# The up-projection's inputs in another column order: feed-forward units by 96-token block, residue and 24 tokens

## The chip, the cores and the metric

The kernel runs on one core of one Trainium2 chip. The metric is the device time of one execution in microseconds (us), lower is better. The engines of a core have queues of their own and work side by side: PE (TensorE, the matmuls; its weight loads, PEld, overlap them), DVE (VectorE), ACT (ScalarE), POOL (GpSimd, which here issues the loads) and SP (SyncE, which here issues the stores and the DMA transposes). Each works through its queue in order.

## The reference

Attention for 8 batches and 8 heads over 576 positions of 64 channels, and a feed-forward block on its 4608 tokens:

```python
mask_plain = (rel >= 0) & (rel < 32)                         # heads 0 to 3
mask_dil = (rel >= 0) & (rel < 128) & (rel % 4 == 0)         # heads 4 to 7
attn = softmax(q @ k.T / 8, under the head's mask) @ v
x = attn.transpose(0, 2, 1, 3).reshape(4608, 512)
a = x @ w1                 # 512 -> 1024
b = x @ w2
out = ((a * b) @ w3) @ w_out
```

`rel` is the query's position less the key's. The inputs are float32; the kernel works in bfloat16 and adds up in float32.

## The kernel before

A batch of attention has four steps (`Step(b, u, hf)`): u = 0 are the plain heads, u = 1 the dilated ones, and hf is a half of the six query blocks of 96. For u = 1 the positions stand by residue modulo 4 (144 of each), so that a dilated window becomes a plain one. A step is: scores on PE (L351, tile `sp`; the two interleaved halves `c` of the 64 channels make a step of two elements between columns of `qt` and `kt`), exponentials on ACT (L361), a mask on DVE (L367; in the first two batches a bias matmul instead, L338), values on PE (L384, tile `vo`), reciprocal and normalisation on DVE (L402, L408, tile `xo`), and a transpose into `XT`: by PE and ACT in batches 0 and 1 (`back`, `keep`), by a DMA transpose from batch 2 on (`back_dma`). `turn` transposes the loaded q, k (and early v) on DVE: in one piece for plain heads (L286), in two for dilated ones (L299), where the write sorts the positions by residue. In batches 0 and 1 `v_back` and `v_keep` bring v into place; later v is loaded in place and `halo_v` (L224) copies the overlap. `band` and `blocks` make the bias at the start, `masks_of_bias` the masks.

`XT[u]` holds, for each partition (two heads of 64 channels), the attention's output: block, head pair, 96 columns. The columns of u = 0 are in the order of the sequence, those of u = 1 by residue.

The feed-forward block works in 16 units of 288 tokens (half a batch: residues 0 and 1, or 2 and 3), each with 8 pairs of groups. A group (`up`, L454, tile `ab`) is four matmuls of 288 columns, one for each 128 of the 512 input channels, in the order `ORDER = (2, 3, 0, 1)`: channels 2 and 3 are of `XT[1]`, 0 and 1 of `XT[0]`. Since a unit is half of the residues, `unit_cols` reads channels 0 and 1 with every fourth column. The first group of a pair is copied by ACT (`copy_a`, L465), the second multiplied with it by DVE (`gate`, L470) into the ring `gt`. `down` (L481, tile `y`) takes 128 tokens of `gt` through w3 @ w_out, which the kernel multiplies once (`w3_back` L511, `w3_keep` L518, `w3_mul` L523, `w3_done` L533); `copy_y` and `store` end the work.

The order on each engine is planned before the program is written: `Plan` runs tasks with given durations and ranks (`RANK`, added to ten times the batch) and takes the ready task of lowest rank. The order found stays fixed. A group is planned at 490 ns. `paced` holds the attention's steps back to about 2.25 batches ahead of the feed-forward block. Where pairs of groups run dry of attention output, or an engine's queue has another task in front, the engine waits.

Of the kernel before, what the change touches and what calls it, by code (L numbers as in the profile page):

```python
# [133 lines left out]
def kernel(  # L134
# [112 lines left out]
    def band():  # L247

        base, mid = bias[:, 1, :], bias[:, 5, QB // 2 : QB]
# [12 lines left out]

    def blocks():

        base = bias[:, 1, :]
        nc.vector.tensor_copy(out=bias[:, 0:5:4, :], in_=base.unsqueeze(1).to_broadcast([P, 2, QB]))
# [3 lines left out]
        nc.vector.tensor_copy(out=bias[:, 6, :], in_=base)  # L270

# [51 lines left out]
    class Step:  # L323
# [8 lines left out]
        def scores(self, biased=False):  # L332
# [12 lines left out]
            for mm in range(3):  # L345
                m = 3 * hf + mm
                for c in range(2):
                    for g in range(4):
                        prt = slice(32 * g, 32 * g + 32)
                        qq = qt[prt, u, QB * m : QB * m + QB, c]  # L350
                        nc.tensor.matmul(  # L351
                            out=self.sp[:, g, QB * mm : QB * mm + QB],
                            lhsT=kt[prt, u, QB * m : QB * m + P, c],
                            rhs=qq,
                            start=(c == 0 and not biased),
                            stop=(c == 1 and (mm == 2 or not biased)),
                        )
# [34 lines left out]
        def recip(self, pg=None):  # L392
            if pg in (None, 0):
                self.rcp = wk_pool.tile([P, 4, 3], F32, tag="rcp", bufs=4, name="rcp")
                self.xo = wk_pool.tile([P, 3, 4, D], BF16, tag="xo", bufs=4, name="xo")
            if pg is None:
# [9 lines left out]
        def norm(self, pg):  # L406
            gs = slice(2 * pg, 2 * pg + 2)
            nc.vector.tensor_tensor(  # L408
                out=self.xo[0:QB, :, gs, :].rearrange("p m g d -> p g m d"),
                in0=self.o[pg][0:QB, :, :, 0:D],  # L410
                in1=self.rcp[0:QB, gs, :].unsqueeze(3).to_broadcast([QB, 2, 3, D]),
                op=AL.mult,
            )

        def cols(self):
            m0 = self.b * BLK + 3 * self.hf
            return XT[self.u][:, m0 : m0 + 3, :, :]

        def back(self):
            self.x = bank([P, 3, 2, QB], BF16, "x")  # L420
            for mm in range(3):
                for pg in range(2):
                    nc.tensor.transpose(  # L423
                        out=self.x[:, mm, pg, :],
                        in_=self.xo[0:QB, mm, 2 * pg : 2 * pg + 2, :],
                        identity=ident[0:QB, 0:QB],
                    )

# [3 lines left out]
        def back_dma(self):  # L432
            nc.sync.dma_start_transpose(
                out=self.cols().rearrange("p m g x -> p (m g) x"),
                in_=self.xo[0:QB, :, :, :].rearrange("p m g d -> p (m g d)"),
            )
# [31 lines left out]
    def gate(k, f):  # L468
        c0 = (k * UNIT) % RING
        nc.vector.tensor_tensor(  # L470
            out=gt[:, f, c0 : c0 + UNIT],
            in0=held[("b", k, f)],
            in1=held[("s", k, f)],
            op=AL.mult,
# [122 lines left out]
    bnd = add("band", "DMA", (700, 0), [c0], band, 2.6, lat=-1800)  # L597
    blk = add("blocks", "DVE", 900, [bnd], blocks, 0, lat=80)
    mk = add("masks", "DVE", 700, [blk], masks_of_bias, 40, lat=80)
# [30 lines left out]
    for b in range(B):  # L630
# [9 lines left out]
        if fast:  # L640
            vals = {}
            for u in range(2):
                tv = turns(b, u, "vn", 10 * b + RANK["T"])
                for half in range(2):
# [4 lines left out]
                    vals[(u, half)] = [  # L649
                        add(f"VK{b}.{u}", eng, 1000, [x, c0],  # L650
                            lambda b=b, u=u, h=half, e=eng: v_keep(b, u, h, e), 10 * b + RANK["VK"], lat=100)
                    ]
        else:
            hal = add(f"HALO{b}", "DVE", 450, LV[b], lambda b=b: halo_v(b), 10 * b + 2, lat=80)
            vals = {(u, h): [hal] + LV[b] for u in range(2) for h in range(2)}
        kept[b], vdone[b] = [], []
        for i in range(4):
# [7 lines left out]
            else:  # L665
                s = add("S" + n, "PE", 480, T[u], st.scores, b - 99 + RANK["S"], after=[prev["s"]])
                e = add("E" + n, "ACT", 1150, [s], st.exps, 10 * b + RANK["E"], lat=100, after=[prev["e"][i]])
                m = add("M" + n, "DVE", 680, [e, mk], st.masks, 10 * b + 2, lat=80)
            paced.append((b, i, s))
            prev["s"] = e  # L670
            ns, rc = [], None
            for pg in range(2):
                vv = add(f"V{n}.{pg}", "PE", 220, [m] + vals[(u, hf)],
                         lambda st=st, pg=pg: st.values(pg), b - 99 + RANK["V"], slot=True)
                rc = add(f"R{n}.{pg}", "DVE", 160, [vv], lambda st=st, pg=pg: st.recip(pg), 10 * b + RANK["N"],
                         lat=0, after=[prev["x"][i], rc])
                ns.append(add(f"N{n}.{pg}", "DVE", 520, [vv, rc], lambda st=st, pg=pg: st.norm(pg),
                              10 * b + RANK["N"], lat=80))
# [16 lines left out]
    def ups(k, f):  # L695
# [14 lines left out]
                 slot=True, after=[a])  # L710
        G[(k, f)] = add("G", "DVE", 453, [bb, ca], lambda: gate(k, f), -1, lat=100)
        gates.append(G[(k, f)])
# [64 lines left out]
```

## Time and profile before

| | |
|---|---|
| runs | 332.85, 333.99, 334.31 us; median 333.99 |
| profiled execution | 333.33 us |
| its span, first to last instruction | 331.5 us |
| mean granted TensorE clock | 0.99 |
| software DMA queue, share of 16 engines' span | 46.0% |
| hardware DMA queue | 18.3% |
| HBM read, written | 38.80 MB, 9.44 MB |

The profile is of one execution. Busy time is the time in which an engine had an instruction at work; a wait is the idle time before an instruction, with what ended it. A group of instructions is told by its line in the kernel, its engine and the tiles it writes and reads (`out<-in`).

### The profile page before, as it was taken

Reading aid. Unit: us, or ns where it says so; the run is one execution under the profiler, and the core shown is the slowest. Engines: PE = TensorE matmul, PEld = TensorE weight load, DVE = VectorE, ACT = ScalarE, POOL = GpSimd, SP = SyncE. Lnnn points to the kernel's source line nnn. Section 1 sums busy time; section 2 is a strip of 40 time slices with the busy share of each in tenths; the row PEclk is TensorE's granted clock in tenths of the full one; section 3 lists DMA queues with packets and bytes.
Section 4 is the critical chain, followed back from the end, with each engine's and each line's share of the span. In section 5 each row is a group of like instructions: output and inputs, shape, how many; then the busy total and the mean of one; then the engine's idle time right before and its main releaser. Section 6 shows DMA issues by size and latency. Waiting matters only on the chain.

```text
span 331.5 us, 6739 instructions
## 1 busy us (share of the span) xinstructions
PE 318.3 (96%) x2706; PEld 177.4 (54%) x2736; DVE 173.0 (52%) x373; ACT 126.5 (38%) x231; POOL 61.5 (19%) x98
## 2 busy tenths in 40 slices
PE   6789999989999999999999999999999999999995
PEld 2565555555555555555555555555555555555552
DVE  5862326997878777876766454444442221222220
ACT  1562254376354333343343332433332232222222
POOL 8413522135432501061122000000000000000000
PEclk9699999999999999999999999999999999999999
DMA  7999999849997959599955131221303110101112
GB/s 111 201 207 208 211 211 130 124 89 149 153 127 122 156 89 159 116 170 143 87 72 69 49 51 50 74 59 29 72 3 81 32 34 36 61 28 35 34 32 95
DMA packets 58030, 32.81 MB, mean 99 GB/s; under 512 B 44688, under 2 KB 47760, under 8 KB 58000
## 3 DMA queue, kind: packets, MB, share of 16 engines
q0 software_dynamic: 37776, 19.40, 46.0%
q1 hardware_dynamic: 20224, 12.98, 18.3%
q8 instruction: 21, 0.34, 0.4%
q14 instruction: 9, 0.07, 0.1%
HBM read 38.80 MB, written 9.44 MB: 145 GB/s over the span
## 4 chain that ended last, share of the span: by engine, by line
PE 92%; DVE 2%; DMA 2%; ACT 2%; issue 1%; POOL 0%; POOLq 0%; ACTq 0%
PE ab L454 59%; PE y L481 18%; PE wf L523 4%; PE sp L351 3%; PE vo L384 3%; DMA vn<-in_v_dram 2%; DVE xo L408 1%; PE sp L338 1%; PE x L511 1%; PE vx L308 1%; ACT et L361 1%; PE x L423 1%; DVE vt L286 0%; ACT asb L465 0%; ACT osb L492 0%
## 5 line engine op out<-in xcount | busy, mean ns | idle before, releaser
L454 PE MATMUL ab<-XT,w_sb 128*128 128x288 bf16 x1024 | 205.1, 360 | 1.2 <-ACT XT L430 0.7
L454 PEld LDWEIGHTS <-w_sb 128*128 128x128 bf16 x1024 | 103.5, 104 | 73.6 <-issue 1.3
L470 DVE TENSOR_TENSOR gt<-ab,asb 128x288 bf16<-128x288 f32 x128 | 58.5, 457 | 123.6 <-PE ab L454 122.8
L465 ACT CAST asb<-ab 128x288 bf16<-128x288 f32 x128 | 51.0, 398 | 107.7 <-PE ab L454 107.2
L481 PE MATMUL y<-wf_sb,gt 128*128 128x512 bf16 x261 | 66.5, 382 | 1.3
L481 PEld LDWEIGHTS <-gt 128*128 128x128 bf16 x288 | 29.3, 102 | 35.3
L492 ACT COPY osb<-y 128x512 f32<-128x512 f32 x36 | 21.1, 585 | 68.4 <-PE y L481 62.1
L361 ACT ACTIVATE et<-sp 128x1152 bf16<-128x1152 f32 x32 | 36.3, 1133 | 15.6 <-PE sp L351 15.4
L217 POOL DMA_DIRECT2D vp<-in_v_dram x48 | 30.3, 637 | 40.5 <-PE vo L384 22.7
L408 DVE TENSOR_TENSOR xo<-vo,rcp 96x384 bf16<-96x384 f32 x64 | 35.0, 551 | 2.1 <-DVE rcp L402 0.2
L384 PEld LDWEIGHTS <-et 128*128 128x128 bf16 x384 | 16.2, 100 | 7.9 <-ACT et L361 1.4
L384 PE MATMUL vo<-vp,et 128*128 128x65 bf16 x384 | 18.0, 197 | 1.4 <-DVE rcp L402 0.6
L367 DVE TENSOR_TENSOR et<-et,mask 128x1152 bf16<-128x1152 bf16 x24 | 17.8, 746 | 0.0
L351 PEld LDWEIGHTS <-kt 32*128 32x128 bf16 x768 | 9.8, 95 | 14.4 <-issue 11.6
L402 DVE RECIPROCAL rcp<-vo 96x6 f32<-96x6 f32 x64 | 11.4, 181 | 9.2 <-PE vo L384 9.1
L351 PE MATMUL sp<-qt,kt 32*128 32x96 bf16 x768 | 14.5, 206 | 0.5 <-DVE kt L286 0.5
L523 PE MATMUL wf<-wo_sb,w3T 128*128 128x512 bf16 x61 | 14.8, 379 | 0.2
L286 DVE STREAM_TRANSPOSE qt<-qn 128x576 uint32<-128x576 uint32 x8 | 10.0, 1246 | 2.9 <-DMA qn<-in_q_dram 2.9
L299 DVE STREAM_TRANSPOSE kt<-kn 128x320 uint32<-128x320 uint32 (+1 forms) x16 | 10.9, 681 | 0.7 <-PE sp L351 0.6
L299 DVE STREAM_TRANSPOSE qt<-qn 128x320 uint32<-128x320 uint32 (+1 forms) x16 | 10.9, 680 | 0.4 <-DMA qn<-in_q_dram 0.2
L518 ACT COPY w3T<-x 128x1024 bf16<-128x1024 bf16 x8 | 8.1, 1012 | 7.1 <-PE x L511 7.0
L195 POOL DMA_DIRECT2D kn<-in_k_dram x9 | 6.0, 671 | 23.7 <-DVE kt L299 22.7
(48 smaller groups left out, 113.7 us busy)
## 6 DMA issues: line engine op xcount, KB each, us to landing
qn<-in_q_dram POOLq DMA_DIRECT2D x7, 576.0 KB, 7.7
kn<-in_k_dram POOLq DMA_DIRECT2D x7, 576.0 KB, 6.9
w_sb<-in_moe_w_dram POOLq DMA_DIRECT2D x4, 512.0 KB, 13.4
w3n<-in_moe_w_dram POOLq DMA_DIRECT2D x8, 256.0 KB, 14.5
out_dram<-osb SPq DMA_DIRECT2D x8, 256.0 KB, 2.4
out_dram<-osb SPq DMA_DIRECT2D x8, 224.0 KB, 2.5
vp<-in_v_dram POOLq DMA_DIRECT2D x6, 288.0 KB, 8.1
out_dram<-osb SPq DMA_DIRECT2D x8, 192.0 KB, 2.3
```

The lines of the kernel that those rows point to most:

```text
L217: nc.gpsimd.dma_start(out=vp[32 + p0 : 32 + p0 + n, 4:8, m, 0:D], in_=v_rows(b, 4, 4 * t0 + res, [[4 * D, n], [S * D, 4], [1, D]]),)
L299: nc.vector.transpose(out=o, in_=i)
L351: nc.tensor.matmul(out=self.sp[:, g, QB * mm : QB * mm + QB], lhsT=kt[prt, u, QB * m : QB * m + P, c], rhs=qq, start=(c == 0 and not biase ...
L361: nc.scalar.activation(out=ev, in_=self.sp[:, :, 0:VC], func=ACT.Exp, scale=scale)
L384: nc.tensor.matmul(out=self.o[g // 2][:, g % 2, mm, :], lhsT=self.et[:, c0 : c0 + P], rhs=vp[:, 4 * self.u + g, 3 * self.hf + mm, 0 : D + ...
L408: nc.vector.tensor_tensor(out=self.xo[0:QB, :, gs, :].rearrange("p m g d -> p g m d"), in0=self.o[pg][0:QB, :, :, 0:D], in1=self.rcp[0:QB, ...
L454: nc.tensor.matmul(out=ps, lhsT=w_sb[:, c, f * P : (f + 1) * P], rhs=unit_cols(k, c), start=(j == 0), stop=(j == DCH - 1),)
L465: nc.scalar.copy(out=a_sb, in_=held[("a", k, f)])
L470: nc.vector.tensor_tensor(out=gt[:, f, c0 : c0 + UNIT], in0=held[("b", k, f)], in1=held[("s", k, f)], op=AL.mult,)
L481: nc.tensor.matmul(out=y, lhsT=gt[:, f, c0 : c0 + P], rhs=wf_sb[:, f, :], start=(f == 0), stop=(f == KFF - 1),)
L492: nc.scalar.copy(out=o_sb, in_=held[("y", i)])
L523: nc.tensor.matmul(out=ps, lhsT=w3T[ft][:, g, :], rhs=wo_sb[:, g, :], start=(g == 0), stop=(g == KFF - 1),)
```

## The change

- The unit's 288 columns are ordered by block of 96 tokens, then residue, then 24 tokens. For u = 0 the query's columns are sorted by residue within a block: `turn` takes q of the plain heads in two pieces, as for the dilated ones, and the scores read `qt` in four runs of 24. `XT[0]` then holds, in each block, the residues one after another, and a unit reads 48 neighbouring columns in each of six blocks.
- For u = 1, `XT[1]` holds one step as a whole (288 columns for each head pair), and a unit reads it as six blocks of two residues of 24 columns. `xo` is written in an order to match: by block, then head, for u = 0; by head pair, block and head for u = 1. `cols`, `back`, `keep` and `back_dma` take a step as 576 flat columns.
- `gate` writes the product back into token order in `gt`: its output is in runs of 24.
- The bias of the plain heads is sorted likewise; `blocks` goes from DVE to ACT, with a memset (`no_halo`) left on DVE.
- One more of the four value copies of batches 0 and 1 goes from ACT to DVE (`VKE`).
- `RANK` and planned durations are other numbers, which only set the order.

```diff
-RANK = dict(E=1.5, VK=2, K=1, N=0.5, T=3, VT=0.4, S=0.1, V=0.4, X=0.4)
+RANK = dict(E=2, VK=1.5, K=1.5, N=0.5, T=3, VT=0.1, S=0.3, V=0.3, X=0.3)
-VKE = (0, 0, 0, 1)
+VKE = (0, 0, 1, 1)
...
-    XT = [const.tile([P, B * BLK, 2, QB], BF16, name=f"XT{u}") for u in range(2)]
+    XT = [
+        const.tile([P, B * BLK, 2, QB], BF16, name="XT0"),
+        const.tile([P, 2 * B, 2, VC], BF16, name="XT1"),
+    ]
...
-        base = bias[:, 1, :]
-        nc.vector.tensor_copy(out=bias[:, 0:5:4, :], in_=base.unsqueeze(1).to_broadcast([P, 2, QB]))
+        base = bias[:, 6, :]
+        by_res = base.rearrange("p (t r) -> p r t", r=4)
+        nc.scalar.copy(
+            out=bias[:, 0:4, :].rearrange("p i (r t) -> p i r t", r=4),
+            in_=by_res.unsqueeze(1).to_broadcast([P, 4, 4, 24]),
+        )
+        nc.scalar.copy(out=bias[:, 4, :], in_=base)
+        nc.scalar.copy(out=bias[:, 5, 0 : QB // 2], in_=base[:, 0 : QB // 2])
+
+    def no_halo():
         nc.vector.memset(bias[0:32, 0:5:4, :], -BIG)
-        nc.vector.tensor_copy(out=bias[:, 2:4, :], in_=base.unsqueeze(1).to_broadcast([P, 2, QB]))
-        nc.vector.tensor_copy(out=bias[:, 5, 0 : QB // 2], in_=base[:, 0 : QB // 2])
-        nc.vector.tensor_copy(out=bias[:, 6, :], in_=base)
...
-                        qq = qt[prt, u, QB * m : QB * m + QB, c]
+                        if u == 0:
+                            qq = qt[prt, u, :, c].rearrange("p (r t) -> p r t", r=4)
+                            qq = qq[:, :, 24 * m : 24 * m + 24]
+                        else:
+                            qq = qt[prt, u, QB * m : QB * m + QB, c]
...
+            if self.u == 0:
+                dst = self.xo[0:QB, :].rearrange("p (m g d) -> p g m d", m=3, g=4)[:, gs, :, :]
+            else:
+                dst = self.xo[0:QB, :].rearrange("p (q m g d) -> p q g m d", q=2, m=3, g=2)
+                dst = dst[:, pg, :, :, :]
...
         def cols(self):
-            m0 = self.b * BLK + 3 * self.hf
-            return XT[self.u][:, m0 : m0 + 3, :, :]
+            if self.u == 0:
+                m0 = self.b * BLK + 3 * self.hf
+                return XT[0][:, m0 : m0 + 3, :, :].rearrange("p m g x -> p (m g x)")
+            return XT[1][:, 2 * self.b + self.hf, :, :].rearrange("p g x -> p (g x)")
...
     def unit_cols(k, c):
         b, hf = k // 2, k % 2
-        x = XT[c // 2][:, b * BLK : (b + 1) * BLK, c % 2, :]
         if c < 2:
-            x = x.rearrange("p m (t r) -> p r m t", r=4)
-            return x[:, 2 * hf : 2 * hf + 2, :, :]
-        return x[:, 3 * hf : 3 * hf + 3, :]
+            return XT[0][:, b * BLK : (b + 1) * BLK, c, 48 * hf : 48 * hf + 48]
+        return XT[1][:, k, c - 2, :].rearrange("p (r m t) -> p m r t", r=2, m=BLK)
...
-            out=gt[:, f, c0 : c0 + UNIT],
-            in0=held[("b", k, f)],
-            in1=held[("s", k, f)],
+            out=gt[:, f, c0 : c0 + UNIT].rearrange("p (r m t) -> p m r t", r=2, m=BLK),
+            in0=held[("b", k, f)].rearrange("p (m r t) -> p m r t", r=2, m=BLK),
+            in1=held[("s", k, f)].rearrange("p (m r t) -> p m r t", r=2, m=BLK),
...
-        parts = (None,) if u == 0 else (0, 1)
+        parts = (None,) if u == 0 and nm != "qn" else (0, 1)
...
-                x = add("XD" + n, "SP", 100, ns, st.back_dma, 0, lat=3000)
+                x = add("XD" + n, "SP", 100, ns, st.back_dma, 0, lat=3700)
```

The order of instructions at two places. First DVE at the start of the program, before (`qt`, `kt`, `vt` are the turned q, k and v of batch 0, `bias` the band of the early batches):

```order
L286 STREAM_TRANSPOSE qt_93<-qn 128x18x32
L266 COPY bias<-bias 128x2x96
L267 MEMSET bias 32x2x96
L268 COPY bias<-bias 128x192
L269 COPY bias<-bias 128x48
L270 COPY bias<-bias 128x96
L286 STREAM_TRANSPOSE kt_91<-kn 128x18x32
L286 STREAM_TRANSPOSE vt_95<-vn 128x18x32
```

And DVE at the same place of the changed kernel:

```order
L309 STREAM_TRANSPOSE qt_93<-qn 128x5x32x2
L309 STREAM_TRANSPOSE qt_93<-qn 128x4x32x2
L296 STREAM_TRANSPOSE kt_91<-kn 128x18x32
L280 MEMSET bias 32x2x96
L283 TENSOR_SCALAR mask<-bias 128x672
L296 STREAM_TRANSPOSE vt_95<-vn 128x18x32
```

The copies of the bias have left DVE, q comes in two pieces, and the memset and the mask stand between k and v.

Second DVE at the end of batch 1's attention, just before batch 2's first mask, before (`rcp` and `xo` are reciprocal and normalisation of one half step, `gt` a gate, `vp<-vp` batch 2's halo):

```order
L402 RECIPROCAL rcp<-vo 96x6
L408 TENSOR_TENSOR xo<-vo,rcp 96x2x3x64
L286 STREAM_TRANSPOSE kt_91<-kn 128x18x32
L299 STREAM_TRANSPOSE kt_91<-kn 128x5x32x2
L224 COPY vp_84<-vp_84 32x8x5x64
L299 STREAM_TRANSPOSE kt_91<-kn 128x4x32x2
L470 TENSOR_TENSOR gt<-ab,asb 128x288
L367 TENSOR_TENSOR et_87<-et_87,mask 128x1152
L470 TENSOR_TENSOR gt<-ab,asb 128x288
```

And in the changed kernel:

```order
L489 TENSOR_TENSOR gt<-ab,asb 128x6x2x24
L416 RECIPROCAL rcp<-vo 96x6
L427 TENSOR_TENSOR xo<-vo,rcp 96x2x3x64
L489 TENSOR_TENSOR gt<-ab,asb 128x6x2x24
L416 RECIPROCAL rcp<-vo 96x6
L427 TENSOR_TENSOR xo<-vo,rcp 96x2x3x64
L416 RECIPROCAL rcp<-vo 96x6
L427 TENSOR_TENSOR xo<-vo,rcp 96x2x3x64
L227 COPY vp_84<-vp_84 32x8x5x64
L381 TENSOR_TENSOR et_87<-et_87,mask 128x1152
```

Gates now stand between the normalisations of batch 1, where before they came behind them. On PE, 96 up-projection matmuls stand ahead of the weight fusion instead of 100, 24 instead of 8 between the first scores of batch 1 and of batch 2, and 420 instead of 432 from there to the third step of batch 6.

More of the change, by code (lines that the diff above doesn't have):

```diff
@@ L247, in band @@
     def band():
-        base, mid = bias[:, 1, :], bias[:, 5, QB // 2 : QB]
+        base, mid = bias[:, 6, :], bias[:, 5, QB // 2 : QB]
         nc.gpsimd.affine_select(
@@ L415, in cols @@
         def cols(self):
-            m0 = self.b * BLK + 3 * self.hf
-            return XT[self.u][:, m0 : m0 + 3, :, :]
+            if self.u == 0:
+                m0 = self.b * BLK + 3 * self.hf
+                return XT[0][:, m0 : m0 + 3, :, :].rearrange("p m g x -> p (m g x)")
+            return XT[1][:, 2 * self.b + self.hf, :, :].rearrange("p g x -> p (g x)")
         def back(self):
[L420 to L427, printed above, removed]
+            self.x = bank([P, 6 * QB], BF16, "x")
+            for i in range(6):
+                nc.tensor.transpose(
+                    out=self.x[:, i * QB : (i + 1) * QB],
+                    in_=self.xo[0:QB, i * P : (i + 1) * P],
+                    identity=ident[0:QB, 0:QB],
+                )
         def keep(self):
@@ L597 @@
     bnd = add("band", "DMA", (700, 0), [c0], band, 2.6, lat=-1800)
-    blk = add("blocks", "DVE", 900, [bnd], blocks, 0, lat=80)
+    blk = add("blocks", "ACT", 1200, [bnd], blocks, 0, lat=100)
+    blk = add("no halo", "DVE", 150, [blk], no_halo, 0, lat=80)
     mk = add("masks", "DVE", 700, [blk], masks_of_bias, 40, lat=80)
@@ L649 @@
                     vals[(u, half)] = [
-                        add(f"VK{b}.{u}", eng, 1000, [x, c0],
+                        add(f"VK{b}.{u}", eng, 1250, [x, c0],
                             lambda b=b, u=u, h=half, e=eng: v_keep(b, u, h, e), 10 * b + RANK["VK"], lat=100)
@@ L653 @@
         else:
-            hal = add(f"HALO{b}", "DVE", 450, LV[b], lambda b=b: halo_v(b), 10 * b + 2, lat=80)
+            hal = add(f"HALO{b}", "DVE", 820, LV[b], lambda b=b: halo_v(b), 10 * b + 2, lat=80)
             vals = {(u, h): [hal] + LV[b] for u in range(2) for h in range(2)}
@@ L667 @@
                 e = add("E" + n, "ACT", 1150, [s], st.exps, 10 * b + RANK["E"], lat=100, after=[prev["e"][i]])
-                m = add("M" + n, "DVE", 680, [e, mk], st.masks, 10 * b + 2, lat=80)
+                m = add("M" + n, "DVE", 750, [e, mk], st.masks, 10 * b + 2, lat=80)
             paced.append((b, i, s))
@@ L674 @@
                          lambda st=st, pg=pg: st.values(pg), b - 99 + RANK["V"], slot=True)
-                rc = add(f"R{n}.{pg}", "DVE", 160, [vv], lambda st=st, pg=pg: st.recip(pg), 10 * b + RANK["N"],
+                rc = add(f"R{n}.{pg}", "DVE", 181, [vv], lambda st=st, pg=pg: st.recip(pg), 10 * b + RANK["N"],
                          lat=0, after=[prev["x"][i], rc])
-                ns.append(add(f"N{n}.{pg}", "DVE", 520, [vv, rc], lambda st=st, pg=pg: st.norm(pg),
+                ns.append(add(f"N{n}.{pg}", "DVE", 551, [vv, rc], lambda st=st, pg=pg: st.norm(pg),
                               10 * b + RANK["N"], lat=80))
@@ L710, in ups @@
                  slot=True, after=[a])
-        G[(k, f)] = add("G", "DVE", 453, [bb, ca], lambda: gate(k, f), -1, lat=100)
+        G[(k, f)] = add("G", "DVE", 460, [bb, ca], lambda: gate(k, f), -1, lat=100)
         gates.append(G[(k, f)])
```

8 lines of the change are left out of this document (4 added, 4 removed).

## The prediction

> **What bounds the kernel now.** I read the page first, then the busy time by stage, then the matrix engine's instructions one line at a time. The page says which engine fills the span (columns: busy us, share of the span, instructions), and which line fills that engine:
>
> ```profile
> span 331.5 us, 6739 instructions
> PE 318.3 (96%) x2706; PEld 177.4 (54%) x2736; DVE 173.0 (52%) x373; ACT 126.5 (38%) x231; POOL 61.5 (19%) x98
> L454 PE MATMUL ab<-XT,w_sb 128*128 128x288 bf16 x1024 | 205.1, 360 | 1.2 <-ACT XT L430 0.7
> L481 PE MATMUL y<-wf_sb,gt 128*128 128x512 bf16 x261 | 66.5, 382 | 1.3
> L470 DVE TENSOR_TENSOR gt<-ab,asb 128x288 bf16<-128x288 f32 x128 | 58.5, 457 | 123.6 <-PE ab L454 122.8
> L465 ACT CAST asb<-ab 128x288 bf16<-128x288 f32 x128 | 51.0, 398 | 107.7 <-PE ab L454 107.2
> ```
>
> PE is the bound: 318.3 of 331.5 us, 205.1 of it in the up-projections of L454, and the readers of its result (gate on DVE, copy on ACT) spend 123 and 107 us waiting for it. But busy is not the same as fast. So next, what one matmul costs. These pieces are from the chain of waits (start, us, what) in the last stage, where PE has nothing but up- and down-projections, and from the timeline of PE (start, us from the first start to the last end):
>
> ```profile
> 302.09 7.60 PE ab L454 x40
> 300.36 1.73 PE y L481 x8
> 300.18 1.91 PE L481 MATMUL y<-wf_sb,gt 128*128 128x512 bf16 x8
> 7.69 0.65 PE L338 MATMUL sp<-bias,ident 128*128 128x288 bf16 x4 [1.35 <-DVE bias L270]
> 8.80 0.44 PE L351 MATMUL sp<-qt,kt 32*128 32x96 bf16 x24 [0.46 <-DVE kt L286]
> L338 PE MATMUL sp<-bias,ident x32: 282/286/448, 7.7 to 69.3; 128*128 128x288 bf16 x32
> L454 PE MATMUL ab<-XT,w_sb x1024: 283/360/440, 22.4 to 321.8; 128*128 128x288 bf16 x171
> ```
> The last two rows are of the views of one line: minimum, median and maximum of one matmul's recorded duration, in ns.
>
> Forty up-projections take 7.60 us: 190 ns each, 760 for a group of four (one output, four channels of 128 inputs). A down-projection of 512 columns takes 1.73/8 = 216 ns, 0.42 ns a column, so 288 columns should take 122. The bias matmuls have exactly that form, 288 columns read in one run: four in 0.65 us, of which the last one's duration is 0.286, so (0.65 - 0.286)/3 = 122. So 760 is not the price of 288 columns. L454 shows two populations: its minimum, 283, is the bias matmul's 282; its maximum is 440; and the median, 360, lies in the gap halfway between, as it must if half of the matmuls are of each kind. The code has the halves: channels 2 and 3 (dilated heads) are read in three runs of 96 columns, channels 0 and 1 (plain heads) in twelve runs of 24 with a step of four elements, 8 bytes. If the first two cost 2 x 122 = 244, the other two cost 516, or 258 each, 2.1 times the price.
>
> **By stage.** The span cut at the first up-projection, the first weight-fusion transpose, the first scores of batch 1, of batch 2, and of the third step of batch 6; then L454 alone in the same stretches:
>
> ```profile
> 0.00:22.40 22.40, 16.30 (x219) 9.96 (x220) 16.29 (x47) 10.29 (x17) 11.69 (x26) 0.85 1.02 169
> 22.40:41.60 19.20, 19.20 (x106) 10.86 (x106) 5.67 (x13) 5.32 (x13) 7.77 (x12) 1.00 1.16 209
> 41.60:60.50 18.90, 18.74 (x134) 10.71 (x136) 9.26 (x13) 8.89 (x10) 4.43 (x7) 1.00 1.15 152
> 60.50:75.30 14.80, 13.65 (x236) 8.88 (x239) 14.01 (x31) 10.13 (x19) 4.68 (x7) 1.00 0.71 123
> 75.30:197.40 122.10, 121.00 (x1183) 67.22 (x1200) 87.92 (x181) 49.60 (x87) 32.97 (x48) 1.00 0.94 115
> 197.40:331.50 134.10, 129.41 (x841) 69.77 (x852) 39.85 (x90) 42.30 (x86) 0.00 (x0) 1.00 0.17 47
> ...
> 22.40:41.60 19.20, 19.11 (x100) 10.40 (x99) 1.00 1.16 209
> 41.60:60.50 18.90, 1.86 (x9) 0.77 (x8) 1.00 1.15 152
> 60.50:75.30 14.80, 1.81 (x8) 0.64 (x8) 1.00 0.71 123
> 75.30:197.40 122.10, 88.10 (x433) 42.41 (x432) 1.00 0.94 115
> 197.40:331.50 134.10, 94.20 (x477) 49.10 (x476) 1.00 0.17 47
> ```
> Columns of the first six: length, busy PE, PEld, DVE, ACT, POOL with their counts, PE's granted clock, DMA share, GB/s. In the second, third, fifth and sixth stage PE is full. In the fourth, DVE is: 14.01 of 14.8 us, 95%. The up-projections stand almost wholly in stages 2, 5 and 6.
>
> **The price of the new read.** After the change channels 0 and 1 are read in six runs of 48 columns, channels 2 and 3 in twelve runs of 24, all with neighbouring elements. Lower end for a group: 4 x 122 = 488. A group that waits at its head pays a little more: the eight y matmuls of the timeline row span 1.91 us, while seven spacings of 0.216 and one duration of 0.382 make 1.89, so some 20 ns. With that, 510. If a group pays it at its head and at its tail, 533. I take 510: the wait stands in both kernels, and the tail's share was seen only behind a stepped read. Against 760 that saves 250 ns a group, 64 us over 256 groups, where PE is what ends last. Does a change of run cost anything? Three runs (L454's 283) against one (L338's 282) say no, to 1 ns; twelve are not in the trace, except with the step.
>
> Here a rule speaks against the change. The Trainium skill, "SBUF — State Buffer", section "Door 1: The DMA port swizzle", says that SBUF has lines of 16 bytes and that two hits in a line give full bandwidth, so that bf16 may be read with a step of up to eight elements for free. By it the 8-byte step costs nothing and the change would save nothing. The trace disagrees: the stepped matmuls are those that take twice as long. Should the rule hold all the same, it must be the twelve runs that cost, and that is a rival below.
>
> What the trace says of steps: the scores (L351) read their columns with a step of two elements, 4 bytes; 24 of them in four concurrent row groups take 0.44 us with the last one's tail of 0.2, so six in turn take 0.24, 40 ns for 96 columns, the full 0.42 ns. So 4 bytes are free. The scores of plain heads now read four runs of 24 with that same step: from nothing to double, 16 steps x 0.24 = 3.8 us; I take nothing, by the step.
>
> **The rest of the change, part by part.** DVE's rows:
>
> ```profile
> L286 DVE STREAM_TRANSPOSE qt<-qn 128x576 uint32<-128x576 uint32 x8 | 10.0, 1246 | 2.9 <-DMA qn<-in_q_dram 2.9
> L299 DVE STREAM_TRANSPOSE qt<-qn 128x320 uint32<-128x320 uint32 (+1 forms) x16 | 10.9, 680 | 0.4 <-DMA qn<-in_q_dram 0.2
> L321 DVE COPY vp<-vx 128x256 bf16<-128x256 bf16 x6 | 2.2, 419 | 0.7 <-PE vx L308 0.7
> L408 DVE TENSOR_TENSOR xo<-vo,rcp 96x384 bf16<-96x384 f32 x64 | 35.0, 551 | 2.1 <-DVE rcp L402 0.2
> 6.72 0.20 DVE L266 COPY bias<-bias 128x192 bf16<-128x192 bf16 x1
> 7.50 1.24 DVE L286 STREAM_TRANSPOSE kt<-kn 128x576 uint32<-128x576 uint32 x1
> ```
> - The plain heads' q is turned in two pieces: 2 x 0.680 for 1.246, +0.11 us in each of 8 batches.
> - The gate writes twelve runs of 24. Norm writes six runs of 64 for 384 elements in 551 ns, gate 288 in 457: 0.98 ns per element between them, with no sign of a price per run. I take 0; should a run cost 5 ns it is 60 ns x 128 = 7.7 us on DVE.
> - Norm writes another order, transposes and keeps the same sizes: nothing. The whole-step DMA transposes write the same 576 columns a partition as now, one piece either way: nothing.
> - Three more value copies on DVE per early batch (+1.26 us there, ACT relieved); the bias blocks (7.50 - 6.72 = 0.8 us of DVE) go to ACT, idle then. The halo memset now stands behind the k transpose, and the first scores' bias matmuls behind it; they waited till 7.69 and PE had the scores at 8.80. Now q's two pieces, k, memset: some 0.3 us later. Against the 0.8 saved: stage 1 stays 22.4, between 21.5 and 23.5.
> - The new ranks and planned durations only reorder. On DVE, gates stand between the normalisations at the start of batch 2; a reciprocal queued there now waits for the up-projection ahead of it, and the values and scores on PE behind their buffers. On PE, 24 groups instead of 25 stand before the weight fusion, 6 instead of 2 in stage 4, 105 instead of 108 in stage 5.
>
> **The sum**, in us:
> 1. Stage 1: 22.4.
> 2. Stage 2: 24 groups x 0.51 + 0.2 = 12.4. The next thing late could be w3, as the fusion now starts at 34.8; its loads:
>
> ```profile
> L511 PE MATMUL x<-ident,w3n 128*128 128x128 bf16 x64 | 4.9, 220 | 0.0
> L243 POOL DMA_DIRECT2D w3n<-in_moe_w_dram x8: 528/530/541, 12.3 to 29.9; - x8
> DMA to landing us min/median/max: 9.8/14.5/18.5
> ```
>    PE never idled for them. The first is there by 12.3 + 18.5 = 30.8 at the latest, the last by 48.4, and its turn comes 7 x 2.2 us into the fusion, at 50: hidden, barely.
> 3. Stage 3: 18.9 - 2 x 0.25 = 18.4; the w3 matmuls bound it.
> 4. Stage 4: DVE-bound, so the two faster groups give nothing; the four moved ones (2.0) fill PE's idle 1.15 and their gates lengthen DVE. PE 13.65 - 0.5 + 2.04 = 15.2. I take 15.3.
> 5. Stage 5: PE 121.0 - 108 x 0.25 - 3 x 0.51 = 92.5. DVE keeps its 87.9, +0.5: a floor of 88.4. DVE at stage 4's 95% would give 93.1. Here the cover is gone: two in-order engines, each at 95%, wait for one another in turn. I add 4 to PE's: 96.5. The upper end is from stage 1, where they chase each other too: 16.29 busy in 22.4 less the 2.9 of its first DMA wait, 84%; 88.4/0.84 = 105.
> 6. Stage 6: 134.1 - 119 x 0.25 = 104.4. Per pair of groups (1.02 us) DVE needs 0.457, ACT 0.398: both hidden.
>
> DMA in stage 5: 0.94 x 122.1 = 115 in 96.5 us is a share of 1.19, just above the 1.16 of stage 2. Loads would slip by 115/1.16 - 96.5 = 3 us; no load is issued in stage 6 today (POOL 0.00), so those of the last batches have that much room. Nothing.
>
> Total 269.4, 62.1 below the span of 331.5. The profiled execution took 333.33, 1.8 beyond its span, and the median of the three runs is 333.99, 0.7 more. Predicted: 269.4 + 1.8 = **271**, on the profiled one's footing.
>
> **Rivals.**
> - *DVE becomes the bound.* Stage 5 at 105 instead of 96.5: 280. For it: 88.4 us of DVE against 92.5 of PE, and gates placed ahead of reciprocals. Against it: DVE reached 95% in stage 4. It decides once DVE idles over 5% there.
> - *Slower: short runs cost, not the step.* If the twelve runs make the 516 ns, 9 runs beyond three cost 516 - 244 = 272 for two matmuls, 15 ns a run. Then channels 2 and 3 cost 516, channels 0 and 1, with six runs, 244 + 2 x 45 = 334; a group 850, 90 more than now: +23 us, 356. A group gets 2 x 9 + 2 x 3 = 24 runs more than four matmuls of three, so it decides above 250/24 = 10 ns a run. Against it: three runs cost no more than one, and the factor is close to two, as a halved rate would give. The rule cited above would make it this case.
> - *Only part of the gain.* Runs of 48 are free, runs of 24 cost half of the excess (68 ns each): a group 646, saving 114 instead of 250, 29 us, so about 305.
> - *No change.* Runs of 24 cost as much as the step did and runs of 48 nothing: 516 + 244 = 760 again, 334.
>
> **How the numbers follow.** The forecast 0.74, DVE 0.13, part 0.06, none 0.02, slower 0.05. The forecast's own range: groups at 488 save 22 ns x 256 = 5.6 more, no stall in stage 5 another 4: 261; groups at 533 cost 5.9, the scores 3.8: 281. With DVE and both above: 288. Range 261 to 288, which holds 0.74 + 0.13 less tails of some 0.05. A measurement here tells about 0.5% (1.7 us) from no change: faster 0.93, same 0.02, slower 0.05.
>
> **What would show it.** L454's busy sum near 135, and its minimum and maximum within some 30 ns of each other; twenty-four of them in 3.1 us in the last stage instead of 4.56. PE still over 92% busy, DVE about 65% of the span, and PE idle for 4 to 10 us in the middle, on DVE. The forecast is wrong if the recorded durations still fall in two kinds (runs cost), or if PE shows long waits for rcp, xo, gt or vp between about 70 and 165 us (DVE bound), or for DMA.

## The result, and the profile after

| | before | after |
|---|---|---|
| median of the runs of this comparison | 334.15 us (332.85 to 334.54, 4 runs) | 265.36 us (264.63 to 267.02, 4 runs) |
| ratio, 95% interval | | 0.795, 0.791 to 0.800 |
| profiled execution, span | 333.33, 331.5 us | 265.60, 263.8 us |

The forecast was 271, between 261 and 288. Of the 16 executions of the unedited changed kernel, in three measurements with medians of 265.36, 267.07 and 264.86 us, those at a mean granted clock of 0.999 or 1.000 took 264.2 to 264.6 us and those at 0.987 took 266.8 to 267.1, while one at 0.85 took 297.4 and enters no ratio.

The page of the changed kernel (busy us, share of the span, instructions; then the up-projection and the gate with mean ns and idle time before them):

```profile
span 263.8 us, 6783 instructions
PE 250.6 (95%) x2736; PEld 168.2 (64%) x2736; DVE 172.6 (65%) x383; ACT 122.3 (46%) x228; POOL 62.7 (24%) x98
L473 PE MATMUL ab<-XT,w_sb 128*128 128x288 bf16 x1024 | 138.0, 286 | 1.2 <-ACT XT L451 0.7
L489 DVE TENSOR_TENSOR gt<-ab,asb 128x288 bf16<-128x288 f32 x128 | 57.9, 454 | 58.0 <-PE ab L473 56.2
```

PE's busy share hardly moved, 96 to 95%, though the kernel does the same work in four fifths of the time: the share says that the engine had a matmul at work, not how fast it was fed. The up-projections lost 67.1 us of busy time (205.1 to 138.0), the span 67.7. DVE's total is the same to 0.4 us, now in a shorter span.

One line's view (minimum, median, maximum ns of a matmul), four pieces of the chain of waits (start, us, what), two of them around the start of stage 5 and two near the end, and a row of PE's timeline:

```profile
L473 PE MATMUL ab<-XT,w_sb x1024: 282/286/297, 23.1 to 254.3; 128*128 128x288 bf16 x171
...
65.52 10.00 DMA vp<-in_v_dram
84.32 3.92 DMA vp<-in_v_dram
...
229.01 4.90 PE ab L473 x40
233.91 1.73 PE y L500 x8
...
233.75 1.89 PE L500 MATMUL y<-wf_sb,gt 128*128 128x512 bf16 x8
```

The two kinds of durations are gone: 282 to 297, where it was 283 to 440. Forty up-projections take 4.90 us instead of 7.60: 122.5 ns each, 490 a group. The channels read in twelve runs of 24 cost the same as those in six runs of 48.

The same six stages, cut at the same instructions (length, busy PE, PEld, DVE, ACT, POOL with counts, granted clock, DMA share, GB/s):

```profile
0.00:23.10 23.10, 15.17 (x218) 9.34 (x219) 17.16 (x47) 10.23 (x17) 11.95 (x26) 0.93 1.02 171
23.10:35.10 12.00, 11.98 (x102) 9.62 (x102) 5.13 (x12) 5.19 (x13) 3.71 (x6) 1.00 1.18 210
35.10:53.50 18.40, 18.40 (x138) 10.64 (x137) 9.66 (x15) 8.55 (x10) 6.37 (x9) 1.00 1.21 206
53.50:67.90 14.40, 13.86 (x237) 9.74 (x235) 13.71 (x31) 9.28 (x17) 5.74 (x8) 1.00 1.10 151
67.90:161.70 93.80, 93.16 (x1195) 63.20 (x1192) 86.62 (x189) 48.14 (x86) 34.95 (x50) 1.00 1.27 149
161.70:263.80 102.10, 98.02 (x853) 65.71 (x852) 40.30 (x93) 40.88 (x86) 0.00 (x0) 1.00 0.26 63
```

| stage | before | forecast | after |
|---|---|---|---|
| 1, start | 22.4 | 22.4 | 23.1 |
| 2, first up-projections | 19.2 | 12.4 | 12.0 |
| 3, weight fusion | 18.9 | 18.4 | 18.4 |
| 4, attention of batch 1 | 14.8 | 15.3 | 14.4 |
| 5, batches 2 to 6 | 122.1 | 96.5 | 93.8 |
| 6, the rest | 134.1 | 104.4 | 102.1 |

Stages 5 and 6 hold 60 of the 68 us gained, stage 2 another 7. PE is full in stages 2, 3, 5 and 6; in the fourth PE and DVE are both at 95 to 96%, and in stage 5 DVE is 92% busy beside PE.

### The profile page after: what moved, and what is told of

Its sections match the earlier page's. It is cut to its first block, busy times and chain, and to the rows that moved or that the text cites. A ratio compares the mean times of both kernels' runs of the same rounds, so it can differ in the third digit from the quotient of the medians.

```text
span 263.8 us, 6783 instructions
## 1 busy us (share of the span) xinstructions
PE 250.6 (95%) x2736; PEld 168.2 (64%) x2736; DVE 172.6 (65%) x383; ACT 122.3 (46%) x228; POOL 62.7 (24%) x98
## 4 chain that ended last, share of the span: by engine, by line
PE 77%; DMA 8%; DVE 7%; issue 3%; POOL 2%; ACT 1%; POOLq 0%; DVEq 0%; ACTq 0%
PE ab L473 43%; PE y L500 20%; DMA vp<-in_v_dram 5%; PE wf L542 5%; PE vo L398 3%; PE sp L365 3%; DMA qn<-in_q_dram 2%; DVE xo L427 1%; DVE qt L309 1%; PE x L530 1%; DVE vp L331 1%; DVE kt L309 1%; POOL vp L220 1%; PE sp L348 1%; PE x L444 1%
## 5 line engine op out<-in xcount | busy, mean ns | idle before, releaser
L473 PE MATMUL ab<-XT,w_sb 128*128 128x288 bf16 x1024 | 138.0, 286 | 1.2 <-ACT XT L451 0.7
L473 PEld LDWEIGHTS <-w_sb 128*128 128x128 bf16 x1024 | 96.5, 98 | 31.2 <-issue 1.7
L489 DVE TENSOR_TENSOR gt<-ab,asb 128x288 bf16<-128x288 f32 x128 | 57.9, 454 | 58.0 <-PE ab L473 56.2
L500 PE MATMUL y<-wf_sb,gt 128*128 128x512 bf16 x288 | 67.7, 379 | 0.6 <-DVE vp L331 0.5
L500 PEld LDWEIGHTS <-gt 128*128 128x128 bf16 x288 | 27.8, 98 | 28.5 <-DVE vp L331 0.7
L220 POOL DMA_DIRECT2D vp<-in_v_dram x48 | 31.4, 659 | 45.8 <-PE vo L398 17.7
L309 DVE STREAM_TRANSPOSE qt<-qn 128x320 uint32<-128x320 uint32 (+1 forms) x32 | 21.5, 681 | 3.3 <-DMA qn<-in_q_dram 3.0
L365 PE MATMUL sp<-qt,kt 32*128 32x96 bf16 x768 | 14.3, 204 | 0.0
L552 DVE CAST wf_sb<-wf 128x512 bf16<-128x512 f32 x8 | 5.5, 692 | 7.4 <-PE wf L542 7.4
L296 DVE STREAM_TRANSPOSE kt<-kn 128x576 uint32<-128x576 uint32 x8 | 9.9, 1240 | 0.0
## 6 DMA issues: line engine op xcount, KB each, us to landing
w3n<-in_moe_w_dram POOLq DMA_DIRECT2D x8, 256.0 KB, 14.3
```

What stands on the lines that cost most here:

```text
L220: nc.gpsimd.dma_start(out=vp[32 + p0 : 32 + p0 + n, 4:8, m, 0:D], in_=v_rows(b, 4, 4 * t0 + res, [[4 * D, n], [S * D, 4], [1, D]]),)
L309: nc.vector.transpose(out=o, in_=i)
L365: nc.tensor.matmul(out=self.sp[:, g, QB * mm : QB * mm + QB], lhsT=kt[prt, u, QB * m : QB * m + P, c], rhs=qq, start=(c == 0 and not biase ...
L473: nc.tensor.matmul(out=ps, lhsT=w_sb[:, c, f * P : (f + 1) * P], rhs=unit_cols(k, c), start=(j == 0), stop=(j == DCH - 1),)
L489: nc.vector.tensor_tensor(out=gt[:, f, c0 : c0 + UNIT].rearrange("p (r m t) -> p m r t", r=2, m=BLK), in0=held[("b", k, f)].rearrange("p ( ...
L500: nc.tensor.matmul(out=y, lhsT=gt[:, f, c0 : c0 + P], rhs=wf_sb[:, f, :], start=(f == 0), stop=(f == KFF - 1),)
```

## The experiments

Each timed run stands beside runs of the kernel before on the same chip; ratios are to those, with a 95% interval.

**The read alone (e_read).** The kernel before with

```diff
         x = XT[c // 2][:, b * BLK : (b + 1) * BLK, c % 2, :]
         if c < 2:
-            x = x.rearrange("p m (t r) -> p r m t", r=4)
-            return x[:, 2 * hf : 2 * hf + 2, :, :]
+            return x[:, :, 48 * hf : 48 * hf + 48]
```

> The kernel before with one edit: channels 0 and 1 are read in six runs of 48 columns from an XT that is still in the order of the sequence, so that a unit is fed other tokens than its own in half of its channels. Nothing else of the change is in it: no second piece of q's transpose, no other order of xo, gate or bias, no other plan. Step theory: all of the gain is in the read, 265 to 269 us. Rival, that the plan's new numbers and the new places of DVE's work carry part of it: 270 to 280 us.

Measured: 267.32 us (265.31 to 268.32), ratio 0.800 (0.796 to 0.805). So this one address pattern carries the gain: it saves 65.5 us, where the whole change saved 65.5 to 68.8 in its three measurements (ratios 0.795, 0.798 and 0.802). All the rest of the change (q in two pieces, the new orders of `xo`, gate and bias, the plan) is what makes the read lawful, since this kernel feeds a unit other tokens than its own; a worth of its own is not shown, as 0.800 lies among the three.

**The step put back (e_step).** The changed kernel with

```diff
         if c < 2:
-            return XT[0][:, b * BLK : (b + 1) * BLK, c, 48 * hf : 48 * hf + 48]
+            x = XT[0][:, b * BLK : (b + 1) * BLK, c, :]
+            x = x.rearrange("p m (t r) -> p r m t", r=4)
+            return x[:, 2 * hf : 2 * hf + 2, :, :]
```

> The changed kernel with one edit: channels 0 and 1 are read again with a step of four elements (from the new XT, so in another order than channels 2 and 3); all the rest of the change stays. Step theory: a group is back near 755 ns, 256 x 0.265 = 68 us over the changed kernel, 330 to 336 us. Rival, that the rest of the change brings a part: under 328 us.

Measured: 333.06 us, ratio 1.000 (0.997 to 1.003). The whole gain is gone. The groups of PE by line, of the read alone and then of the step put back:

```profile
L453 PE MATMUL ab<-XT,w_sb 128*128 128x288 bf16 x1024 | 138.7, 288 | 2.9 <-DVE xo L408 1.9 <-ACT XT L430 0.7
```
```profile
L475 PE MATMUL ab<-XT,w_sb 128*128 128x288 bf16 x1024 | 206.1, 360 | 1.0 <-ACT XT L451 0.7
```

With the step 206 us, without it 138, whatever layout and plan stand around it.

**What a read costs by itself (e_probe).** No attention and no feed-forward; 32 matmuls for each way of reading:

```python
reads["step_four"] = t[:, :, 0]          # t is [128, 288, 4]; likewise 1, 2, 3, 5, 6, 8, 16
reads["run_of_twelve"] = t[:, :, 0:12]   # t is [128, 24, 24]; likewise 48, 24, 6, 4, 2
for i in range(32):
    nc.tensor.matmul(out=ps[i % 4][:, 0:288], lhsT=w, rhs=r, start=True, stop=True)
```

> This kernel computes nothing of the reference: it runs 32 matmuls of 288 columns for each way of reading the moving operand (one element in 1, 2, 3, 4, 5, 6, 8, 16; unbroken runs of 48, 24, 12, 6, 4, 2 elements with gaps as long; the old read of channels 0 and 1), and then groups of two plain reads and two of the old kind. Step theory: 122 ns for a step of one and two elements, 240 for four and for the old read, and 122 for runs of 48 and 24. What it does beyond that is open: a rate by bytes would give 122 x step/2 (180 at three elements, 490 at eight, 980 at sixteen); a rate that falls once to a half would give 240 for all from three on. Line theory (two hits in 16 bytes are enough): 122 up to four elements, and dearer only from five on. For short runs: if each run is fetched in pieces of 8 bytes, runs of 4 and longer are free and runs of 2 behave like a step. Alternation theory: in the mixed groups the old reads cost about 22 ns more than by themselves, 760 a group, and the plain reads behind them as well; otherwise 2 x 122 + 2 x 238 = 720.

The timeline of PE (start, us from the first start to the last end, what); the spacing of one matmul is the difference of two starts, over 32:

```profile
12.70 4.08 PE L60 MATMUL ps<-step_one,w 128*128 128x288 bf16 x32
16.62 4.24 PE L60 MATMUL ps<-step_two,w 128*128 128x288 bf16 x32
20.69 6.34 PE L60 MATMUL ps<-step_three,w 128*128 128x288 bf16 x32
26.87 8.34 PE L60 MATMUL ps<-step_four,w 128*128 128x288 bf16 x32
35.04 10.39 PE L60 MATMUL ps<-step_five,w 128*128 128x288 bf16 x32
45.25 12.41 PE L60 MATMUL ps<-step_six,w 128*128 128x288 bf16 x32
57.48 16.45 PE L60 MATMUL ps<-step_eight,w 128*128 128x288 bf16 x32
73.75 16.75 PE L60 MATMUL ps<-step_sixteen,w 128*128 128x288 bf16 x32
90.32 6.56 PE L60 MATMUL ps<-run_of_fortyeight,w 128*128 128x288 bf16 x32
96.71 4.08 PE L60 MATMUL ps<-run_of_twentyfour,w 128*128 128x288 bf16 x32
100.63 4.08 PE L60 MATMUL ps<-run_of_twelve,w 128*128 128x288 bf16 x32
104.55 5.07 PE L60 MATMUL ps<-run_of_six,w 128*128 128x288 bf16 x32
109.45 4.24 PE L60 MATMUL ps<-run_of_four,w 128*128 128x288 bf16 x32
113.53 4.22 PE L60 MATMUL ps<-run_of_two,w 128*128 128x288 bf16 x32
117.59 8.37 PE L60 MATMUL ps<-old,w 128*128 128x288 bf16 x32
125.78 0.42 PE L63 MATMUL ps<-step_one,w 128*128 128x288 bf16 x2
...
126.54 0.43 PE L63 MATMUL ps<-step_one,w 128*128 128x288 bf16 x2
```

Steps of 1, 2, 3, 4, 5, 6, 8 and 16 elements cost 122, 127, 193, 255, 319, 382, 508 and 518 ns: 64 ns for each element of step above two, and a plateau at eight. The old read costs what a plain step of four costs (256), so its twelve runs add nothing; runs of 24 and 12 are free, those of four and two take 127, and those of six 153. A mixed group takes 126.54 - 125.78 = 0.76 us, which is 2 x 122 + 2 x 256 = 756: near the alternation theory's 760, but because the old read costs 256 by itself. The alternation costs nothing.

That is not a rate halved once, as I had put it, nor a rate by bytes, which would have no plateau. One size fits all eight steps to within 2%: a read of 288 columns with a step of s elements of 2 bytes touches 36 s lines of 16 bytes, and 288 lines from a step of eight on; at 1.78 ns a line that is 128, 192, 256, 320, 384, 512, 512. The columns themselves need 122. Lines of 16 bytes are what the Trainium skill, "SBUF — State Buffer", section "Door 1: The DMA port swizzle", has too. Its rule that two hits in a line give full bandwidth does not hold here: with two hits (step four) the price is 255 instead of 122, with 2.7 (step three) 193, and only with four (step two) 127. That lines are the mechanism is inferred from this fit; the short runs below do not follow it.

**The plateau, the clock and odd runs (e_probetwo).** The first probe's granted clock fell to a half during step six, and its runs of 48 stand at the end of that stretch (6.56 us). So a second one puts twenty plain matmuls ahead of eight of each read:

```diff
+        for i in range(20):
+            nc.tensor.matmul(out=ps[i % 4], lhsT=w, rhs=warm, start=True, stop=True)
-        for i in range(32):
+        for i in range(8):
             nc.tensor.matmul(out=ps[i % 4][:, 0:N], lhsT=w, rhs=r, start=True, stop=True)
```

> This kernel computes nothing of the reference. Twenty plain matmuls of 512 columns stand ahead of each read's eight matmuls of 288 columns, so that the granted clock should stay full. Line theory, from the first probe (64 ns per element of step up to eight, then 509 to 518): what costs is each 16-byte line that the read touches, 1.78 ns of it, unless the 122 ns of the columns are longer. It gives 128 for a step of two, 256 for four, 512 for eight, sixteen and thirty-two alike; 122 for runs of 36, 18, 9 and 8, 128 for runs of three, and 128 for runs of six, where the first probe measured 153 for reasons not known; 122 for a plain read that starts at an odd element. Byte theory (the span between first and last byte at 9 bytes a ns) gives 1020 for sixteen and 2040 for thirty-two. Theory that the halved clock of the first probe made the plateau: eight to thirty-two differ from 509 to 518 once the clock is full.

The timeline of PE; the spacing is (us less the last one's duration) over seven, and the durations are 0.685, 0.698 and 0.660 for the steps, and for the runs of 18, 9, 6 and 3 and the odd start 0.292, 0.306, 0.318, 0.324 and 0.287:

```profile
23.97 4.22 PE L61 MATMUL ps<-step_eight,w 128*128 128x288 bf16 x8
...
32.34 4.30 PE L61 MATMUL ps<-step_sixteen,w 128*128 128x288 bf16 x8
36.47 6.18 PE L59 MATMUL ps<-warm,w 128*128 128x512 bf16 x20
42.48 4.03 PE L61 MATMUL ps<-step_thirtytwo,w 128*128 128x288 bf16 x8
...
57.65 1.20 PE L61 MATMUL ps<-run_of_eighteen,w 128*128 128x288 bf16 x8
...
63.01 1.32 PE L61 MATMUL ps<-run_of_nine,w 128*128 128x288 bf16 x8
...
73.77 1.38 PE L61 MATMUL ps<-run_of_six,w 128*128 128x288 bf16 x8
...
79.31 1.46 PE L61 MATMUL ps<-run_of_three,w 128*128 128x288 bf16 x8
...
84.93 1.15 PE L61 MATMUL ps<-odd_start,w 128*128 128x288 bf16 x8
```

Steps of 8, 16 and 32 cost 505, 515 and 481, each at a granted clock of 1.00: the plateau is no work of the clock, and a rate by bytes is out (2040 for 32). Line theory gives 512 for all three; the 6% at 32 are unexplained. A plain read from an odd element costs 123, as expected. Line theory is wrong for some short runs: those of 18, nine, six and three elements cost 130, 145, 152 and 162 where it gives 122 to 128, while runs of 8, 12, 24, 36 and 48 are free. None of the dear lengths is a multiple of four elements, as 24 and 48 in the changed kernel are; but two is none either, and costs 127. Why is open.

**The plan without the layout, and the layout without the plan (e_newplan, e_oldplan).**

```diff
-RANK = dict(E=1.5, VK=2, K=1, N=0.5, T=3, VT=0.4, S=0.1, V=0.4, X=0.4)
-VKE = (0, 0, 0, 1)
+RANK = dict(E=2, VK=1.5, K=1.5, N=0.5, T=3, VT=0.1, S=0.3, V=0.3, X=0.3)
+VKE = (0, 0, 1, 1)
```

and the planned durations of the change's diff: put into the kernel before, and the other way round into the changed one.

> The kernel before with the changed kernel's planning numbers (RANK, VKE and planned durations) and nothing of its layout. Step theory: PE is full behind stepped reads, so the order hardly matters: 334 us, within 1.5. Rival, that the numbers are worth something by themselves: 327 to 331 us.

Measured: 335.91 us, ratio 1.008 (1.006 to 1.011). Without the layout the new numbers cost about 2.7 us (2.0 to 3.5 by the interval), which neither theory had: the order is not quite without effect when PE is full.

> The changed kernel's layout with the planning numbers of the kernel before (RANK, VKE, planned durations). In the layout of before, the new numbers made 335.9 of 332.8, 0.8% slower. Theory that PE is full and the numbers hardly matter: within 1.5 us of the changed kernel. Theory that they matter only now, when DVE is 92% busy in the middle stage: 268 to 272 us. Theory that the new numbers cost what they cost before (a third value copy on DVE, and their order): 262 to 263 us.

Measured: 268.04 us, ratio 0.805 (0.802 to 0.808). The measure for it, the unedited changed kernel:

> The changed kernel itself, unedited, as the measure for the three others of this call: 265.4 us, ratio 0.795 to the kernel before.

Measured: 267.07 us, ratio 0.802 (0.799 to 0.805). The old numbers are 1 us behind, with intervals that overlap, which fits both of the first two theories. That the new ones still cost what they cost before (262 to 263) is out; whether they bring a microsecond now is not resolved.

**One value copy back on ACT (e_vke).**

```diff
-VKE = (0, 0, 1, 1)
+VKE = (0, 0, 0, 1)
```

> The changed kernel with VKE as before: in batches 0 and 1 the third of four value copies is ACT's again, six copies of 0.41 us less on DVE, three of them in stage 1. Stage 1 lasted 23.1 us instead of 22.4, so if DVE bounds it: 264 to 265 us, 0.5 to 1.5 less than the changed kernel. If ACT's copies come later than DVE's would: the same or 1 us more.

Measured: 267.99 us, ratio 0.804 (0.801 to 0.807), beside 0.802. The 264 to 265 us of a stage 1 bound by DVE did not come, and the difference to 0.802 lies within the intervals. In its trace the first up-projection stands at 22.5 us, in that of the unedited kernel beside it at 22.8.

**More work for DVE (e_dve).** The changed kernel with its mask instruction issued twice:

```diff
             nc.vector.tensor_tensor(out=ev, in0=ev, in1=mk, op=AL.mult)
+            nc.vector.tensor_tensor(out=ev, in0=ev, in1=mk, op=AL.mult)
```

> The changed kernel with each of the 24 masks multiplied in twice (the mask is of zeros and ones, so nothing changes but the time): 24 x 0.752 = 18 us more on DVE, about 20 of the 24 in stage 5, which has 86.6 us of DVE in 93.8. Theory that DVE's queue is the next bound at once, at the 92 to 95% of fill it has reached: stage 5 becomes (86.6 + 15)/0.92 to 0.95 = 107 to 110, the whole 278 to 282 us. Theory that DVE's bound is soft, because attention runs 2.25 batches ahead of the feed-forward block and its work can slip into stage 6, where DVE is 40% busy: under 273 us.

Measured: 274.82 us, ratio 0.825 (0.822 to 0.828): 7.8 us over the unedited kernel's 267.07 for 18 us of added DVE work. Stages 5 and 6 of its trace, columns as above, and the longest of PE's waits (in all, times, longest):

```profile
67.40:170.30 102.90, 96.26 (x1194) 61.80 (x1192) 98.47 (x207) 48.25 (x86) 34.51 (x50) 1.00 1.12 136
170.30:272.90 102.60, 98.53 (x853) 65.45 (x852) 44.91 (x99) 40.87 (x86) 0.00 (x0) 1.00 0.25 62
...
PE vo L399 <- DVE et L382: 3.3, 8, 0.8
```

Both theories miss in the number; the mechanism is nearer to a full queue. The bound is not soft (under 273): stage 6 took up no more of the work than its own six masks. The 278 to 282 counted on 15 us more in stage 5; 18 of the masks stand there, not 20, and DVE's busy time rose by 11.9. With that, a fill of 95% would make 98.5/0.95 = 103.7 us; the stage took 102.9, a fill of 96%. At that fill DVE bounds a stage of 93.8 us from about 89.8 us of work on, so the changed kernel, with 86.6, stands some 3 us of DVE work from that point. This is an estimate from one dose; a smaller one was not run.

**The start (e_start, e_again_two).** The changed kernel with the halo memset planned ahead of q's transpose and the mask behind the first v:

```diff
-    bnd = add("band", "DMA", (700, 0), [c0], band, 2.6, lat=-1800)
-    blk = add("blocks", "ACT", 1200, [bnd], blocks, 0, lat=100)
+    bnd = add("band", "DMA", (700, 0), [c0], band, 2.6, lat=-3600)
+    blk = add("blocks", "ACT", 300, [bnd], blocks, 0, lat=100)
...
-    mk = add("masks", "DVE", 700, [blk], masks_of_bias, 40, lat=80)
+    mk = add("masks", "DVE", 700, [blk, L[("vn", 0, 0)]], masks_of_bias, 40, lat=80)
```

> The changed kernel with three planning numbers of the start changed, so that DVE does the bias's halo memset ahead of q's transpose, and the mask behind the first v. PE waited 2.0 us for that memset, and the first scores came at 9.1 us. If that wait is on the path: the first scores at 8.3 to 8.5, and 0.5 to 0.8 us less in all, 264.5 to 265. If stage 1 is bound by the landing of v (9.1) and DVE's queue behind it: no change, and the first up-projection still at 23.1.

> The changed kernel itself, unedited, as the measure for the one before it: 265 to 267 us.

Measured: 265.04 us (264.03 to 265.57), ratio 0.797 (0.796 to 0.799), beside the unedited kernel's 264.86 (264.17 to 267.13), 0.798 (0.795 to 0.800). The timeline of PE in e_start has the first scores at 8.34:

```profile
8.34 0.44 PE L365 MATMUL sp<-qt,kt 32*128 32x96 bf16 x24 [0.44 <-DVE kt L296]
```

The first up-projection of its trace comes at 21.9, 1.2 us earlier than the 23.1 of the unedited one, and the profiled span is 262.6 against 263.8. Not all of that is the edit: the mean granted clock of this stage is 1.00 in its trace and 0.93 in the other, where four bias matmuls at 15.78 us took 1.15 us instead of 0.65. Ahead of that stretch the edited kernel's second scores are 0.4 us early (11.31 against 11.70), behind it the fourth 1.2 (18.12 against 19.34). The timed runs do not show a gain: the medians differ by 0.2 us the other way, within their scatter. A gain of the size expected is neither shown nor excluded, so there is no version here that is shown to beat the changed kernel.

## Why the prediction was right, point by point

- *The two kinds of matmul.* Right. The median of durations halfway between two populations, and a price of 2.1 for half of them, pointed at the step; putting it back alone gave the old time, taking it away alone gave the new one.
- *The rule of lines, and the rival built on it.* The twelve runs cost nothing (282 to 297 ns for all 1024 matmuls), so the slower rival and the partial one fell at once. The probe shows what the trace of before could not: the price grows with the step up to eight elements, as if each line of 16 bytes had one.
- *The price of a group.* The mis-sized term. I took 510 and its lower end, 488, was the truth (490). The 20 ns that I added for a wait at the head came from a y group's row, 1.91 us against 1.89. In the changed kernel the same row spans 1.89: the surcharge stood only behind a stepped read. The mixed groups of the probe show that it was no time lost: two plain matmuls behind two stepped ones span 0.42 to 0.43 us there, where one spacing and one duration make 0.41, and yet the whole group takes no more than its four reads, 756 ns. 256 x 0.02 = 5.1 us is most of the 5.6 us between the forecast span of 269.4 and 263.8, and all of the 2.3 us by which stage 6 was forecast too long.
- *Stage 5.* The 4 us added for two nearly full engines were mostly something else. With groups at 490 PE's share would be 92.5 - 105 x 0.02 = 90.4; the stage took 93.8, so 3.4 of the 4 us seem to be there. Only about 1.7 of them are waits, by the starts of the up-projections: so much do their spacings exceed 122.5 ns, without the 95 ns ahead of each step's scores, which the kernel before pays too (111 there). Another 0.6 us are twelve transposes of batch 1 that the new order puts into this stage. And 1.1 us is where I started too low, from the 121.0 us busy of a stage of 122.1: its row counts 1183 matmuls beside 1200 weight loads, so some matmuls have no record and read as idle time. Of the 1.7 us PE's list of waits in that stage holds 0.2: a matmul's recorded 286 ns spans more than twice its spacing of 122, and hides gaps of up to some 160 ns. So the 4 to 10 us in which PE was to idle on DVE did not come, nor did DVE as the bound (280); by the estimate from e_dve some 3 us more of DVE work would have begun it.
- *DMA.* A share of 1.19 was expected to exceed the 1.16 seen before and cost nothing. It rose to 1.27; that 1.16 was a ceiling was wrong, and the trace of before already had 1.25 between 80 and 100 us. It cost PE little, but not for certain nothing: around the start of stage 5 the chain of waits now runs through two loads of v, of 10.0 and 3.9 us, and some of the 1.7 us of gaps stand there (up to 0.36 us each).
- *Stages 1 to 4.* Stage 1 is within its bounds (23.1 of 21.5 to 23.5), but 0.7 longer where I had it unchanged: PE's first scores came 0.3 later, as forecast, behind a wait of 2.0 us for the memset (1.4 before), and DVE had 0.9 us more to do there (17.16 for 16.29); the 1.26 us of the three value copies were not in my sum for this stage. The fusion took 18.4 as computed, stage 4 0.9 less than forecast. One slip is in the range: 271 + 8.5 + 5.9 + 3.8 makes 289, not 288, and nothing hangs on it.
- *Free parts.* The gate with runs of 24 took 454 ns instead of 457, the halves of q 681 as priced; and the scores' four runs of 24 at the 4-byte step kept PE's score matmuls at 14.3 us (14.5 before).

## What to carry to other kernels

A matrix engine that is 95% busy may still be fed at half its rate: divide a stretch of matmuls by their number and columns, compare with a plain one, and look for two populations of durations in one line. Lay a moving operand out so that columns read one after another are neighbours, or two elements apart at most in bfloat16; runs of 8, 12, 24, 36 and 48 elements cost nothing here, but runs of 18 cost 7% and runs of three a third more. It may pay to move the sort to the writers: here a transposing write, a gate and a bias took it over for nothing that these runs could measure.

## What the runs showed of the hardware that was not expected

- The price of a stepped read grows evenly with the step: 127, 193, 255, 319, 382, 508 ns for 288 columns at 2, 3, 4, 5, 6 and 8 elements; from there to 32 it stays within 481 to 518.
- It is a price in time, not in PE's clocks. With the clock halved, steps of 8 and 16 took the 508 and 518 ns that they took with it full (505, 515), while the starts of the runs of 48 lie 240 ns apart at the halved clock and 122 once it is full again.
- The granted clock fell in stretches of slow reads. These are stretches of the first probe from step four on (length, busy PE, PEld, DVE, POOL, granted clock, DMA share, GB/s):

```profile
27.00:35.00 8.00, 8.00 (x33) 3.56 (x31) 0.00 (x0) 0.00 (x0) 1.00 0.00 0
35.00:45.50 10.50, 10.50 (x34) 3.82 (x33) 0.00 (x0) 0.00 (x0) 1.00 0.00 0
45.50:58.00 12.50, 12.50 (x34) 3.96 (x33) 0.00 (x0) 0.00 (x0) 0.58 0.01 1
58.00:74.00 16.00, 16.00 (x33) 4.04 (x32) 0.00 (x0) 0.00 (x0) 0.50 0.00 0
```

  PE counts as fully busy in each, and yet in the third the granted clock falls to a half. In the second probe the twenty plain matmuls behind eight of step sixteen took 6.18 us instead of 4.50, at a mean granted clock of 0.71, and those behind step 32 likewise; behind step eight they took 4.50. What sets the clock is not shown beyond that. The kernel before, where every second pair of reads is plain, kept 0.99.
